# TensorE's scores in an inner loop with addresses computed up front, loops without `head_slot`, and an identity matmul moved ahead, in a decode-attention kernel

## The chip, the cores and the metric

The kernel runs on one core of one Trainium2 chip. The metric is the device time of one execution in microseconds (us), as the median of several runs. All runs quoted here are of the fast state, with a granted TensorE clock of 1.0. A profiled span is about 1.3 us shorter than the device time of the same run.

## The reference

One query per head attends to 65,536 keys: 32 query heads share 8 key and value heads, of dimension 128, in bf16.

```python
B, Hq, Hkv, Sq, Sk, D = 1, 32, 8, 1, 65536, 128
def reference(q, k, v):
    k = jnp.repeat(k, rep, axis=1)          # rep = 4
    v = jnp.repeat(v, rep, axis=1)
    scores = jnp.einsum("bhqd,bhkd->bhqk", q, k) * D ** -0.5
    p = _softmax(scores, axis=-1)
    return jnp.einsum("bhqk,bhkd->bhqd", p, v)
```

K and V together are 268 MB, and every byte is used once.

## The kernel before

K and V are cut into 16 tiles each (N = 16; two tiles per head), of 8.39 MB. The kernel keeps two K tiles and one V tile on the chip. SyncE issues the loads. A K tile may be loaded when VectorE has transposed the tile that lay there, and a V tile when TensorE has finished the product with the V tile before (PV).

```python
def load_k(i):
    if i >= NK: sp.wait_ge(tr_s, (i - NK + 1) * G)
    ...
def load_v(i):
    if i < N - HALVED:
        if i >= 1: sp.wait_ge(pv_s, 2 * i)
        load(vbuf, vf, i, 0, T, v_in)
        return
    ...                                      # the last two tiles are loaded in halves and pieces
load_k(0)
for j in range(1, N + 1):
    if j < N: load_k(j)
    load_v(j - 1)
```

On TensorE a turn of the loop makes the scores of tile `it`, 16 groups of 16 products, all unrolled, then the 256 small products with V of tile `it - 1`. `head_slot` in the head of a loop asks for a place for the loop's first instruction, slot 0 here; all three compute engines use it.

```python
with nc.Fori(0, N + 1, 1, engines=..., head_slot={pe.engine: 0}) as it:
    ...
    with pe.If_lt(turn, N):
        for g in range(G):
            if g % GU == 0: pe.wait_ge(mv_s, it * U + (g // GU + 1))
            pe.wait_ge(tr_s, it * G + (g + 1))
            scores(g, qcols)                 # 16 matmuls
    with pe.If_eq(skip, 0):
        pe.wait_ge(ex_s, it * R); pe.wait_ge(v_in, whole_ * 16)   # cut
        values(range(TH)); ...               # PV
pe.wait_ge(tail_s, 2)
pe.matmul(acc[:, 0:R], lhsT=ident, rhs=o2, start=False, stop=False)   # fp32 identity, in the tail
for n, a, b in list(pieces(VLAST, TH))[-NEND:]:                        # last 16 and 8 tiles of V
    pe.wait_ge(vlast_in[n], 16)
    values(range(a, b))
# VectorE and ScalarE:
with nc.Fori(0, H, 1, engines=..., head_slot={dv.engine: 0}) as h: ...
with nc.Fori(0, H, 1, engines=..., head_slot={ac.engine: 0}) as h: ...
```

Of the kernel before, what the change touches and what calls it, by code (L numbers as in the profile page):

```python
# [5 lines left out]
DT = mybir.dt  # L6
AF = mybir.ActivationFunctionType
ALU = mybir.AluOpType
AX = mybir.AxisListType

P = 128
S4 = 32
T = 256
TG = 16
G = T // TG
U = 4
GU = G // U
NK = 2
NKT = 2
FIRST = (64, 64, 128)  # L20
KLAST = (128, 128)
VLAST = (72, 32, 16, 8)
NEND = 2
HALVED = 2


# [8 lines left out]
def bass_standalone__gqa_softmax__decode_kernel(nc, q, k, v, out):  # L35
    B, Hq, Sq, D = q.shape
    _, H, Sk, _ = k.shape
    R = Hq // H
    CK = P * T
    assert B == 1 and Sq == 1 and D == P and Hq == H * R == S4 and R == 4  # L40
    C = Sk // CK
    assert Sk % CK == 0 and C == 2
    N = H * C
    A = P // S4
    NB, NE = 2, 2
    W = T // U * R
    TH = T // 2
    QH = NB * NE * A * R
    scale = float(D) ** -0.5
    TE = sum(VLAST[-NEND:])  # L50
# [6 lines left out]
    S = es.enter_context  # L57
# [6 lines left out]
    ktb = [sb(f"ktb{i}", [P, TG * D], DT.bfloat16) for i in range(NKT)]  # L64
    scs = sb("scs", [P, T * R], DT.float32)
    pts = sb("pts", [P, T * R], DT.bfloat16)
    qblk = sb("qblk", [P, H * QH], DT.bfloat16)
# [14 lines left out]
    dif, wgt, rhead, lsum, recip, o1, o2 = (cols(R) for _ in range(7))  # L82
# [5 lines left out]
    q4, qt = (scs[:, i * D // 2:(i + 1) * D // 2].bitcast(DT.bfloat16) for i in range(2))  # L88
    ident = ktb[0][:, 0:2 * P].bitcast(DT.float32)

    qkb = [S(nc.psum_tensor(f"qkb{i}", [P, 512], DT.float32)) for i in range(U)]
    acc = S(nc.psum_tensor("acc", [P, 512], DT.float32))

    def sem(name):
# [19 lines left out]
    def pieces(sizes, at=0):  # L114
        for n, size in enumerate(sizes):
            yield n, at, at + size
            at += size
# [66 lines left out]

    @block.tensor
    def _(pe):
        def scores(g, qcols):


            kt = ktb[g % NKT][:, :].rearrange("p (b n e) -> p b e n", b=NB, e=NE)  # L190
            for n in range(TG // A):
                at = (g % GU * (TG // A) + n) * A * R
                for be in range(NB * NE):
                    ins = pe.matmul(  # L194
                        qkb[g // GU][:, at:at + A * R],
                        lhsT=kt[:, be // NE, be % NE, n * P:(n + 1) * P],
                        rhs=qblk[:, bass.ds(qcols[be], A * R)],
                        start=be == 0, stop=be == NB * NE - 1,
                    )
            ins.then_inc(qk_s, 1)  # L200

        def values(tiles):

            for t in tiles:
                ins = pe.matmul(  # L205
                    acc[:, 0:R], lhsT=vbuf[:, t * D:(t + 1) * D], rhs=pts[:, t * R:(t + 1) * R],
                    start=t == 0, stop=t == T - 1,
                )
                if t % TH == TH - 1:
                    ins.then_inc(pv_s, 1)  # L210


        turn, skip, skipl, late, last, kept, whole = (
            pe.alloc_register(name) for name in ("turn", "skip", "skipl", "late", "last", "kept", "whole"))
        pe.reg_mov(turn, 0)
        pe.wait_ge(qb_s, A * NB)
        with nc.Fori(
            0, N + 1, 1, engines=bass.OrderedEngineSet([pe.engine]), head_slot={pe.engine: 0},
        ) as it:
            pe.reg_alu(skip, it, 1, ALU.is_lt)  # L220
            pe.reg_alu(last, it, N, ALU.is_ge)
            pe.reg_alu(late, it, N - HALVED + 1, ALU.is_ge)
            pe.reg_add(skipl, skip, last)
            pe.reg_alu(kept, it, N - 1, ALU.min)
            pe.reg_alu(whole, it, N - HALVED, ALU.min)
            kept_ = pe.snap(kept, min_val=0, max_val=N - 1)
            whole_, late_, last_ = (pe.snap(r, min_val=0, max_val=N) for r in (whole, late, last))
            hq = kept_ // C * QH
            qcols = [hq + be * A * R for be in range(NB * NE)]
            with pe.If_lt(turn, N):  # L230
                for g in range(G):
                    if g % GU == 0:
                        pe.wait_ge(mv_s, it * U + (g // GU + 1))
                    pe.wait_ge(tr_s, it * G + (g + 1))
                    scores(g, qcols)
            with pe.If_eq(skip, 0):
                pe.wait_ge(co_s, it - 1)
                pe.wait_ge(ex_s, it * R)
                pe.wait_ge(v_in, whole_ * 16)
                pe.wait_ge(va_in, late_ * 16 + last_ * 16)  # L240
                values(range(TH))
                pe.wait_ge(vb_in, late_ * 16)
                for n, a, b in list(pieces(VLAST, TH))[:-NEND]:
                    pe.wait_ge(vlast_in[n], last_ * 16)
                    values(range(a, b))
            with pe.If_eq(skipl, 0):
                values(range(T - TE, T))
            pe.reg_add(turn, turn, 1)


        pe.wait_ge(tail_s, 2)
        pe.wait_ge(ow_s, H)
        pe.matmul(acc[:, 0:R], lhsT=ident, rhs=o2, start=False, stop=False)  # L253
        for n, a, b in list(pieces(VLAST, TH))[-NEND:]:
            pe.wait_ge(vlast_in[n], 16)
            values(range(a, b))

    @block.vector
    def _(dv):
# [47 lines left out]
            dv.alloc_register(name) for name in ("started", "before", "filled", "last"))  # L307


        with nc.Fori(0, H, 1, engines=bass.OrderedEngineSet([dv.engine]), head_slot={dv.engine: 0}) as h:  # L310
            dv.reg_alu(started, h, 1, ALU.is_ge)
            dv.reg_alu(last, h, H - 1, ALU.is_ge)
            dv.reg_alu(filled, h, 1, ALU.add)
            dv.reg_alu(filled, filled, H - 1, ALU.min)
            dv.reg_alu(before, h, -1, ALU.add)
            dv.reg_alu(before, before, 0, ALU.max)
            started_, last_ = dv.snap(started, min_val=0, max_val=1), dv.snap(last, min_val=0, max_val=1)
            filled_, before_ = dv.snap(filled, min_val=0, max_val=H - 1), dv.snap(before, min_val=0, max_val=H - 2)
            for b in range(C):
                dv.wait_ge(k_in[b], (filled_ if b else h) * 16)  # L320
                moved = h * (C * U) + (U + b * U + 1)
                for g in range(G):
                    for n, at, _ in pieces(KLAST if b else FIRST):
                        if at == g * TG:
                            dv.wait_ge((klast_in if b else first_in)[n], last_ * 16 if b else 16)
                    if b * G + g >= NKT:
                        dv.wait_ge(qk_s, h * (C * G) + (b * G + g - NKT + 1))  # L327
                    else:
                        dv.wait_ge(qk_s, h * (C * G) - started_ * (NKT - 1 - g))  # L329
                    transpose(b, g)  # L330
                    if g >= 2 * GU and g % GU == 0:
                        maximum(b, g // GU - 2, moved)
                for u in range(U - 2, U):
                    maximum(b, u, moved)
                dv.wait_ge(mx_s, h * (C * U) + (b + 1) * U)
                if b:
                    dv.wait_ge(hma_s, h * C + 1)
                dv.tensor_reduce(  # L338
                    hmax[:, b * R:(b + 1) * R], hp[b].rearrange("p (u g) -> p g u", g=R), AX.X, ALU.max,
                ).then_inc(hm_s, 1)  # L340
                if b:
                    dv.wait_ge(hma_s, h * C + 2)
                    dv.tensor_tensor(dif, mfirst, mtot, ALU.subtract).then_inc(df_s, 1)  # L343
                    dv.wait_ge(pv_s, h * (2 * C) + 2)
                    dv.tensor_copy(o1, acc[:, 0:R]).then_inc(co_s, 1)  # L345
                else:
                    with dv.If_eq(started, 1):
                        weigh(before_)
                        dv.wait_ge(pv_s, h * (2 * C))
                        dv.wait_ge(ow_s, h)  # L350
                        dv.tensor_tensor(o2, acc[:, 0:R], o2, ALU.add).then_inc(co_s, 1)  # L351
                        divisor(before_)
                        dv.wait_ge(co_s, h * C)
                        dv.tensor_tensor(oT[:, bass.ds(before_ * R, R)], o2, recip, ALU.mult).then_inc(fin_s, 1)  # L354
# [9 lines left out]
    def _(ac):  # L364
# [4 lines left out]
        ac.activation(warm[:, 8:9], warm[:, 9:10], AF.Exp, scale=1.0).then_inc(warm_s, 1)  # L369

        def move(b, u):
            fr = qkb[u][:, 0:W].rearrange("p (n a g) -> p a n g", a=A, g=R)
            to = scs[:, u * W:(u + 1) * W].rearrange("p (n x g) -> p x n g", x=A, g=R)
            for x in range(A):
                for a in range(A):
                    ins = ac.activation(to[a * S4:(a + 1) * S4, x, :, :], fr[x * S4:(x + 1) * S4, a, :, :], AF.Copy)  # L376
            ins.then_inc(mv_s, 1)


        with nc.Fori(0, H, 1, engines=bass.OrderedEngineSet([ac.engine]), head_slot={ac.engine: 0}) as h:  # L380
            for b in range(C):
                ac.wait_ge(ex_s, h * (C * R) + b * R)
                for u in range(U):
# [49 lines left out]
```

## Time and profile before

| | before |
|---|---|
| time, median of 3 runs | 629.17 us (629.02 to 629.17) |
| span of the profiled run | 628.1 us |
| last V data landed (trace) | 625.04 us |
| first transpose of K on VectorE | 18.54 us |
| second V load issued | 78.1 us |

These are lines of the profile's page: busy time by engine, the span in 40 slices with the load rate, and the DMA queues (packets, MB, share of the 16 DMA engines' time). The queues marked "instruction" carry the instruction fetches. In the packet records of the span those of q8 have 16 KB and take 0.97 to 1.07 us, those of q14 have 8 KB and take 0.31 to 0.32 us. A fetch, or a block, is below one such packet. I put q8 down to TensorE and q14 to the other engines.

```profile
span 628.1 us, 19282 instructions
PE 269.9 (43%) x8194; PEld 243.9 (39%) x8194; DVE 341.2 (54%) x411; ACT 275.6 (44%) x1178; POOL 10.5 (2%) x32
...
DMA  9999999999999999999999999999999999999997
GB/s 368 438 449 424 439 422 413 455 413 451 417 451 417 451 417 442 426 442 426 438 430 438 430 434 434 434 434 434 430 438 430 438 430 430 438 415 430 434 432 293
...
q1 hardware_dynamic: 5892, 268.45, 99.1%
q8 instruction: 5, 0.08, 0.1%
...
q14 instruction: 5, 0.04, 0.0%
```

The DMA engines are busy from the first slice to the last, and no compute engine is busy much over half of the time. From the landing times of the loads, a tile takes 19.35 us in steady state. That is 8.389 MB / 19.35 us = 433.5 GB/s.

The waits of VectorE for its transposes (total us, times, longest):

```profile
DVE ktb L276 <- DMA kbuf<-in_k_dram: 142.3, 16, 11.5
...
DVE ktb L276 <- PE qkb L194: 7.0, 1, 7.0
DVE ktb L276 <- issue: 6.0, 1, 6.0
```

VectorE waits for data in every tile (16 waits, 142.3 us in all): here the loads set the pace. The other two waits come once each, near the start. The 6.0 us lie before the first transpose, and an 8 KB block is fetched within them, at 16.0 us (0.31 us).

The window from 78 to 81 us, where the second V load is issued (the last number is GB/s):

```profile
core 0: us, PE busy (x) PEld busy (x) DVE busy (x) ACT busy (x) POOL busy (x), PEclk, DMA share, GB/s
78.00:81.00 3.00, 0.04 (x2) 0.00 (x0) 0.16 (x1) 2.92 (x8) 0.00 (x0) 1.00 0.79 284
```

The chain of waits from 564 us to the end (start, length, what):

```profile
574.46 30.99 DMA vbuf<-in_v_dram
...
605.49 3.59 PE acc L205 x128
...
609.47 13.69 DMA vbuf<-in_v_dram
...
623.20 1.01 PE acc L205 x32
624.21 0.02 issue
624.23 0.56 PE acc L253 x2
624.79 0.69 PE acc L205 x24
```

The 0.56 us piece is the identity matmul. It sits on the drawn chain, but the last 8 of the 24 products behind it have to wait for data that landed at 625.04 us.

The trace records 16 increments of a load's semaphore, and the page counts 16 DMA engines; I read each increment as the landing of one DMA engine's share. The 16 times of a load then show how far the DMA engines are apart. For the second K tile they run from 41.64 to 43.80 us: the last DMA engine is 2.16 us behind the first. Below, this distance is called the lag. The times carry no name of a DMA engine, so "the last" is whichever one comes last in a load.

### The profile page before, as it was taken

How to read it: one execution, taken by the hardware profiler on the slowest of the kernel's cores; microseconds unless marked ns; L12 is line 12 of the kernel's file. 1: busy time of each engine (PE TensorE's matmuls, PEld its weight loads, DVE VectorE, ACT ScalarE, POOL GpSimd, SP SyncE). 2: the span in 40 equal slices, each digit the busy share in tenths (PEclk: the TensorE clock that was granted, in tenths of full speed). 3: DMA queues.
4: the chain of work that ended last, by engine and by line, in shares of the span. 5: the costliest groups of instructions: out<-in, count | busy, mean ns of one | idle time of the engine just before them, and what ended most of it. 6: DMA issues, size and time to landing. Idle time of an engine off the chain costs nothing.

```text
span 628.1 us, 19282 instructions
## 1 busy us (share of the span) xinstructions
PE 269.9 (43%) x8194; PEld 243.9 (39%) x8194; DVE 341.2 (54%) x411; ACT 275.6 (44%) x1178; POOL 10.5 (2%) x32
## 2 busy tenths in 40 slices
PE   0323737144361534615346252452615526156445
PEld 0312636044361433614335152452514526146444
DVE  1865576290753908538094480935719357195910
ACT  0363645164351734517346172461725526264640
POOL 0000000000000000000000000000000000000000
DMA  9999999999999999999999999999999999999997
GB/s 368 438 449 424 439 422 413 455 413 451 417 451 417 451 417 442 426 442 426 438 430 438 430 434 434 434 434 434 430 438 430 438 430 430 438 415 430 434 432 293
DMA packets 6094, 268.60 MB, mean 428 GB/s; under 512 B 964, under 2 KB 964, under 8 KB 1220
## 3 DMA queue, kind: packets, MB, share of 16 engines
q1 hardware_dynamic: 5892, 268.45, 99.1%
q8 instruction: 5, 0.08, 0.1%
q10 hardware_dynamic: 192, 0.03, 0.0%
q14 instruction: 5, 0.04, 0.0%
HBM read 268.47 MB, written 0.01 MB: 427 GB/s over the span
## 4 chain that ended last, share of the span: by engine, by line
DMA 63%; DVE 16%; issue 10%; PE 10%; DVEq 0%; SPq 0%; ACTq 0%
DMA kbuf<-in_k_dram 55%; DVE ktb L276 14%; PE acc L205 9%; DMA vbuf<-in_v_dram 7%; DVE small L283 1%; DMA scs<-in_q_dram 1%; PE qkb L194 1%; SPq L124 0%; ACTq L366 0%; DVE qblk L271 0%; DVEq L329 0%; DVEq L327 0%; PE acc L253 0%; DVE scs L263 0%; DVE oTX L361 0%
## 5 line engine op out<-in xcount | busy, mean ns | idle before, releaser
L276 DVE STREAM_TRANSPOSE ktb<-kbuf 128x1024 int32<-128x1024 int32 x256 | 295.7, 1212 | 155.8 <-DMA kbuf<-in_k_dram 142.3
L376 ACT ACTIVATE scs<-qkb 32x64 f32<-32x64 f32 x1024 | 220.3, 215 | 280.2 <-PE qkb L194 269.0
L194 PE MATMUL qkb<-qblk,ktb 128*128 x4096 | 157.1, 176 | 341.4 <-DVE ktb L276 326.4
L194 PEld LDWEIGHTS qkb<-qblk,ktb 128*128 128x128 bf16 x4096 | 132.7, 105 | 365.7 <-issue 202.6
L205 PE MATMUL acc<-pts,vbuf 128*128 128x4 bf16 x4096 | 112.4, 166 | 14.1 <-DMA vbuf<-in_v_dram 13.4
L205 PEld LDWEIGHTS acc<-pts,vbuf 128*128 128x128 bf16 x4096 | 111.0, 104 | 15.7 <-DMA vbuf<-in_v_dram 11.6
L283 DVE TENSOR_REDUCE small<-scs 128x4 f32<-128x256 f32 x64 | 37.5, 586 | 61.4 <-ACT scs L376 61.4
L399 ACT ACTIVATE pts<-scs,small 128x256 bf16<-128x256 f32 x64 | 48.9, 853 | 30.7 <-PE acc L205 30.5
L171 POOL PARTITION_ALL_REDUCE small<-small x16 | 5.9, 370 | 589.9 <-DVE small L338 589.9
L399 ACT ACTIVATION_READ_ACCUMULATOR pts<-scs,small 128x1 f32 x64 | 13.6, 213 | 0.0
L387 ACT ACTIVATE small<-small 128x4 f32<-128x4 f32 x16 | 3.3, 206 | 22.5 <-POOL small L171 22.5
L345 DVE COPY small<-acc 128x4 f32<-128x4 f32 x8 | 1.3, 161 | 19.4 <-PE acc L205 19.4
L351 DVE TENSOR_TENSOR small<-acc,small 128x4 f32<-128x4 f32 x7 | 1.1, 163 | 13.8 <-PE acc L205 13.8
L359 DVE TENSOR_TENSOR oTX<-acc,small 128x4 bf16<-128x4 f32 x1 | 0.2, 163 | 12.3 <-PE acc L205 12.3
L263 DVE STREAM_TRANSPOSE scs<-scs 128x64 int32<-128x64 int32 x1 | 0.2, 246 | 9.8 <-DMA scs<-in_q_dram 9.8
L338 DVE TENSOR_REDUCE small<-small 128x4 f32<-128x16 f32 (+1 forms) x16 | 3.0, 185 | 1.3
L163 POOL PARTITION_ALL_REDUCE small<-small x8 | 3.4, 429 | 11.5 <-DVE small L296 11.5
L343 DVE TENSOR_TENSOR small<-small 128x4 f32<-128x4 f32 x8 | 1.3, 163 | 4.0 <-POOL small L171 4.0
L294 DVE TENSOR_TENSOR small<-small 128x4 f32<-128x4 f32 x8 | 1.3, 163 | 2.7 <-ACT pts L399 2.7
L369 ACT ACT_TABLE_LOAD x1 | 1.3, 1283 | 3.1 <-issue 3.1
L354 DVE TENSOR_TENSOR oTX<-small 128x4 f32 x7 | 1.1, 163 | 1.7 <-DVE small L300 1.7
L292 DVE TENSOR_TENSOR small<-small 128x4 f32<-128x4 f32 x8 | 1.4, 181 | 0.9
(18 smaller groups left out, 8.8 us busy)
## 6 DMA issues: line engine op xcount, KB each, us to landing
kbuf<-in_k_dram SPq DMA_DIRECT2D x3, 4096.0 KB, 40.2
vbuf<-in_v_dram SPq DMA_DIRECT2D x3, 4096.0 KB, 24.7
kbuf<-in_k_dram SPq DMA_DIRECT2D x2, 2048.0 KB, 10.3
vbuf<-in_v_dram SPq DMA_DIRECT2D x1, 2304.0 KB, 11.6
vbuf<-in_v_dram SPq DMA_DIRECT2D x1, 1024.0 KB, 13.7
vbuf<-in_v_dram SPq DMA_DIRECT2D x1, 512.0 KB, 14.5
vbuf<-in_v_dram SPq DMA_DIRECT2D x1, 256.0 KB, 14.6
kbuf<-in_k_dram SPq DMA_DIRECT2D x14, 49.8
```

The source lines that it names most:

```text
L163: g.partition_all_reduce(lsum, rhead, P, bass.bass_isa.ReduceOp.add).then_inc(ls_s, 1)
L171: g.partition_all_reduce(mtot if b else mfirst, hmax[:, b * R:(b + 1) * R], P, bass.bass_isa.ReduceOp.max,).then_inc(hma_s, 1)
L194: ins = pe.matmul(qkb[g // GU][:, at:at + A * R], lhsT=kt[:, be // NE, be % NE, n * P:(n + 1) * P], rhs=qblk[:, bass.ds(qcols[be], A * R)] ...
L205: ins = pe.matmul(acc[:, 0:R], lhsT=vbuf[:, t * D:(t + 1) * D], rhs=pts[:, t * R:(t + 1) * R], start=t == 0, stop=t == T - 1,)
L276: dv.transpose(to.rearrange("p (b t j) -> p b t j", b=NB, t=TG), fr.rearrange("p (t b i) -> p b t i", b=NB, t=TG),).then_inc(tr_s, 1)
L283: dv.tensor_reduce(hp[b][:, u * R:(u + 1) * R], scs[:, u * W:(u + 1) * W].rearrange("p (n g) -> p g n", g=R), AX.X, ALU.max,).then_inc(mx_ ...
L292: dv.tensor_tensor(o2, o1, wgt, ALU.mult).then_inc(ow_s, 1)
L294: dv.tensor_tensor(rhead, rsum[0], wgt, ALU.mult).then_inc(rw_s, 1)
L338: dv.tensor_reduce(hmax[:, b * R:(b + 1) * R], hp[b].rearrange("p (u g) -> p g u", g=R), AX.X, ALU.max,).then_inc(hm_s, 1)
L376: ins = ac.activation(to[a * S4:(a + 1) * S4, x, :, :], fr[x * S4:(x + 1) * S4, a, :, :], AF.Copy)
L387: ac.activation(negb[b], mtot if b else mfirst, AF.Copy, scale=-scale).then_inc(nb_s, 1)
L399: ac.activation(pv[:, g_, :], sv[:, g_, :], AF.Exp, bias=negb[b][:, g_:g_ + 1], scale=scale, accum_out=rsum[b][:, g_:g_ + 1],).then_inc(ex ...
```

## The change

The intent was to shrink TensorE's program: the scores become an inner loop of 8 turns with two groups each, and the addresses of a turn are put into registers before its first wait. An empty first turn of the outer loop walks through the code while the data is still on its way. `head_slot` is gone from all three loops; VectorE's and ScalarE's then stay where they fall. The identity matmul moves from the tail into the middle of the last PV.

```diff
-qkb = [S(nc.psum_tensor(f"qkb{i}", [P, 512], DT.float32)) for i in range(U)]
+qkb = S(nc.psum_tensor("qkb", [P, U * BANK], DT.float32))
 ...
-        with nc.Fori(0, N + 1, 1, engines=..., head_slot={pe.engine: 0}) as it:
-            with pe.If_lt(turn, N):
-                for g in range(G):
-                    if g % GU == 0:
-                        pe.wait_ge(mv_s, it * U + (g // GU + 1))
-                    pe.wait_ge(tr_s, it * G + (g + 1))
-                    scores(g, qcols)
+        with nc.Fori(0, N + 2, 1, engines=engines) as it:
+            with pe.If_eq(skipk, 0):
+                addresses(qs)
+                with nc.Fori(0, G // NKT, 1, engines=engines) as gp:
+                    outs = [products(at + n * TG * R) for n in range(NKT)]
+                    addresses(sum(outs, []))
+                    pe.wait_ge(mv_s, kb_ * U + (upto + 1))
+                    for n in range(NKT):
+                        pe.wait_ge(tr_s, kb_ * G + (gp * NKT + (n + 1)))
+                        scores(ktb[n], outs[n], qs)
 ...                                    # PV in four parts, each under its own If
+                        with pe.If_eq(last, 1):
+                            pe.wait_ge(tail_s, 2)
+                            pe.wait_ge(ow_s, H)
+                            pe.matmul(acc[:, 0:R], lhsT=ident, rhs=o2, start=False, stop=False)
-        pe.wait_ge(tail_s, 2)
-        pe.wait_ge(ow_s, H)
-        pe.matmul(acc[:, 0:R], lhsT=ident, rhs=o2, start=False, stop=False)
 ...
-        with nc.Fori(0, H, 1, engines=..., head_slot={dv.engine: 0}) as h:
+        with nc.Fori(0, H, 1, engines=...) as h:
-        with nc.Fori(0, H, 1, engines=..., head_slot={ac.engine: 0}) as h:
+        with nc.Fori(0, H, 1, engines=...) as h:
```

More of the change, by code (lines that the diff above doesn't have):

```diff
@@ L23 @@
 NEND = 2
+BANK = 512
+PVIF = 4
 HALVED = 2
@@ L186, in _, with addresses, products, scores @@
     def _(pe):
-        def scores(g, qcols):
-            kt = ktb[g % NKT][:, :].rearrange("p (b n e) -> p b e n", b=NB, e=NE)
-            for n in range(TG // A):
-                at = (g % GU * (TG // A) + n) * A * R
-                for be in range(NB * NE):
+        def addresses(aps):
+            for ap in aps:
+                pe.lower_ap(ap)
+        def products(at):
+            return [qkb[:, bass.ds(at + n * A * R, A * R)] for n in range(TG // A)]
+        def scores(kt, outs, qs):
+            kt = kt[:, :].rearrange("p (b n e) -> p b e n", b=NB, e=NE)
+            for n, o in enumerate(outs):
+                for be, q_ in enumerate(qs):
                     ins = pe.matmul(
-                        qkb[g // GU][:, at:at + A * R],
-                        lhsT=kt[:, be // NE, be % NE, n * P:(n + 1) * P],
-                        rhs=qblk[:, bass.ds(qcols[be], A * R)],
+                        o, lhsT=kt[:, be // NE, be % NE, n * P:(n + 1) * P], rhs=q_,
                         start=be == 0, stop=be == NB * NE - 1,
@@ L210, in values @@
                     ins.then_inc(pv_s, 1)
-        turn, skip, skipl, late, last, kept, whole = (
-            pe.alloc_register(name) for name in ("turn", "skip", "skipl", "late", "last", "kept", "whole"))
-        pe.reg_mov(turn, 0)
-        pe.wait_ge(qb_s, A * NB)
-        with nc.Fori(
-            0, N + 1, 1, engines=bass.OrderedEngineSet([pe.engine]), head_slot={pe.engine: 0},
-        ) as it:
-            pe.reg_alu(skip, it, 1, ALU.is_lt)
-            pe.reg_alu(last, it, N, ALU.is_ge)
-            pe.reg_alu(late, it, N - HALVED + 1, ALU.is_ge)
-            pe.reg_add(skipl, skip, last)
-            pe.reg_alu(kept, it, N - 1, ALU.min)
-            pe.reg_alu(whole, it, N - HALVED, ALU.min)
-            kept_ = pe.snap(kept, min_val=0, max_val=N - 1)
-            whole_, late_, last_ = (pe.snap(r, min_val=0, max_val=N) for r in (whole, late, last))
-            hq = kept_ // C * QH
-            qcols = [hq + be * A * R for be in range(NB * NE)]
-            with pe.If_lt(turn, N):
-                for g in range(G):
-                    if g % GU == 0:
-                        pe.wait_ge(mv_s, it * U + (g // GU + 1))
-                    pe.wait_ge(tr_s, it * G + (g + 1))
-                    scores(g, qcols)
-            with pe.If_eq(skip, 0):
-                pe.wait_ge(co_s, it - 1)
-                pe.wait_ge(ex_s, it * R)
-                pe.wait_ge(v_in, whole_ * 16)
-                pe.wait_ge(va_in, late_ * 16 + last_ * 16)
-                values(range(TH))
-                pe.wait_ge(vb_in, late_ * 16)
-                for n, a, b in list(pieces(VLAST, TH))[:-NEND]:
-                    pe.wait_ge(vlast_in[n], last_ * 16)
-                    values(range(a, b))
@@ new lines, in _ @@
+        engines = bass.OrderedEngineSet([pe.engine])
+        turn, skip, skipk, skipl, late, last, kb, vb, whole = (
+            pe.alloc_register(name)
+            for name in ("turn", "skip", "skipk", "skipl", "late", "last", "kb", "vb", "whole"))
+        with nc.Fori(0, N + 2, 1, engines=engines) as it:
+            pe.reg_add(turn, it, 0)
+            pe.reg_alu(skip, it, 2, ALU.is_lt)
+            pe.reg_alu(last, it, N + 1, ALU.is_ge)
+            pe.reg_alu(skipk, it, 1, ALU.is_lt)
+            pe.reg_add(skipk, skipk, last)
+            pe.reg_alu(late, it, N - HALVED + 2, ALU.is_ge)
+            pe.reg_add(skipl, skip, last)
+            pe.reg_alu(kb, it, -1, ALU.add)
+            pe.reg_alu(kb, kb, 0, ALU.max)
+            pe.reg_alu(kb, kb, N - 1, ALU.min)
+            pe.reg_alu(vb, it, -1, ALU.add)
+            pe.reg_alu(vb, vb, 0, ALU.max)
+            pe.reg_alu(whole, vb, N - HALVED, ALU.min)
+            kb_ = pe.snap(kb, min_val=0, max_val=N - 1)
+            vb_, whole_, late_, last_ = (pe.snap(r, min_val=0, max_val=N) for r in (vb, whole, late, last))
+            with pe.If_eq(skipk, 0):
+                pe.wait_ge(qb_s, A * NB)
+                hq = kb_ // C * QH
+                qs = [qblk[:, bass.ds(hq + be * A * R, A * R)] for be in range(NB * NE)]
+                addresses(qs)
+                with nc.Fori(0, G // NKT, 1, engines=engines) as gp:
+                    upto = gp // (GU // NKT)
+                    at = gp * (NKT * TG * R) + upto * (BANK - W)
+                    outs = [products(at + n * TG * R) for n in range(NKT)]
[4 more added lines that the diff above has]
+                        scores(ktb[n], outs[n], qs)
+            parts = [range(n * T // PVIF, (n + 1) * T // PVIF) for n in range(PVIF)]
+            parts[-1] = range(parts[-1][0], T - TE)
+            for n, part in enumerate(parts):
+                with pe.If_eq(skip, 0):
+                    if n == 0:
+                        pe.wait_ge(co_s, vb_ - 1)
+                        pe.wait_ge(ex_s, vb_ * R)
+                        pe.wait_ge(v_in, whole_ * 16)
+                        pe.wait_ge(va_in, late_ * 16 + last_ * 16)
+                    if part[0] == TH:
+                        pe.wait_ge(vb_in, late_ * 16)
+                        with pe.If_eq(last, 1):
+                            pe.wait_ge(tail_s, 2)
+                            pe.wait_ge(ow_s, H)
+                            pe.matmul(acc[:, 0:R], lhsT=ident, rhs=o2, start=False, stop=False)
+                    at = part[0]
+                    for m, a, b in list(pieces(VLAST, TH))[:-NEND]:
+                        if a in part:
+                            values(range(at, a))
+                            pe.wait_ge(vlast_in[m], last_ * 16)
+                            at = a
+                    values(range(at, part[-1] + 1))
@@ L246, in _ @@
             with pe.If_eq(skipl, 0):
                 values(range(T - TE, T))
-            pe.reg_add(turn, turn, 1)
-        pe.wait_ge(tail_s, 2)
-        pe.wait_ge(ow_s, H)
-        pe.matmul(acc[:, 0:R], lhsT=ident, rhs=o2, start=False, stop=False)
         for n, a, b in list(pieces(VLAST, TH))[-NEND:]:
@@ L307, in _ @@
             dv.alloc_register(name) for name in ("started", "before", "filled", "last"))
-        with nc.Fori(0, H, 1, engines=bass.OrderedEngineSet([dv.engine]), head_slot={dv.engine: 0}) as h:
+        with nc.Fori(0, H, 1, engines=bass.OrderedEngineSet([dv.engine])) as h:
             dv.reg_alu(started, h, 1, ALU.is_ge)
@@ L371, in move @@
         def move(b, u):
-            fr = qkb[u][:, 0:W].rearrange("p (n a g) -> p a n g", a=A, g=R)
+            fr = qkb[:, u * BANK:u * BANK + W].rearrange("p (n a g) -> p a n g", a=A, g=R)
             to = scs[:, u * W:(u + 1) * W].rearrange("p (n x g) -> p x n g", x=A, g=R)
@@ L377, in move @@
             ins.then_inc(mv_s, 1)
-        with nc.Fori(0, H, 1, engines=bass.OrderedEngineSet([ac.engine]), head_slot={ac.engine: 0}) as h:
+        with nc.Fori(0, H, 1, engines=bass.OrderedEngineSet([ac.engine])) as h:
             for b in range(C):
```

## The prediction

> **What bounds the kernel.** The DMA engines. The page's slices show DMA busy 9 tenths throughout, 413 to 455 GB/s in the middle; from landing times one 8.39 MB tile takes 19.35 us (433.5 GB/s), so 32 tiles take 619 of the span's 628.1 us. [...] TensorE is busy 43%, VectorE 54%. The chain of waits names VectorE and TensorE only because their work ends in the next DMA issue; but a V load lands 31 us after its issue, a K load 50 us, against 19.35 us for its own bytes, so a V issue has about 11 us to spare. Compute is off the critical path except at the start and end.
>
> **What the change does.**
> 1. TensorE's 512 score instructions per tile become 64 in a loop of 8 turns, with an empty first outer turn. The DMA records show TensorE fetching five 16 KB instruction blocks (at 16.2, 31.6, 41.6, 48.6, 55.9 us, about 1.05 us each), and in the second tile VectorE waits 7.0 us once for scores. [...] I expect three or four, earlier.
> 2. [...] VectorE idles 6.0 us for "issue" from 12.5 us, with a fetch at 16.0. I expect the first transpose at 13 to 14 us.
> 3. Each pair of groups computes eight addresses and branches: estimate 0.5 to 1.5 us, from 0.046 us per register operation in the trace. TensorE's pair takes 1.2 us of VectorE's 2.3 to 2.8 us, so it is nearly hidden: at most 2 us later per tile.
> 4. The fp32 identity matmul (0.56 us in the tail) moves ahead. But the last 8 weight tiles start at 625.08, right after the last landing at 625.04: at most 0.05 us gained.
>
> **What is critical.** At 78.1 us V's second load is issued when only 2.3 us of earlier data are left for the fastest DMA engine; 78 to 81 us runs at 284 GB/s, losing about 1.0 us of mean engine time. With steps 1 and 2 the first PV ends some 6 to 12 us sooner and this dip goes. But the completion counts show the slowest engine already 2.1 us behind the fastest at 44 us, and it lost only about 0.15 us in the dip. The last engine decides, so I credit 0.1 to 0.3 us. At the end, V halves are issued with 1 to 3 us to spare (issue at 600.6, the load before landing 603.5 to 605.4 us), so a slower TensorE could cost up to 1 us.
>
> **Prediction.** 628.8 us, 8 in 10 between 627.9 and 629.9. Chances: faster by over 2% 0.01, within 2% 0.98, slower 0.01.
>
> **What would show it.** GB/s per slice unchanged after the sixth; V's second load issued before 73 us, without a dip; first transpose before 15 us; fewer 16 KB instruction packets; VectorE's wait for K near 140 us; last landing to the span's end still about 3 us.
>
> **What would make it wrong.** [...] more instruction packets, microseconds of "issue" per tile, single DMA engines delayed. Or addresses cost over 9 us per tile, and the DMA rate dips each period.

The marked gaps, here and in the expectations below, are statements that no trace or run of this case shows. 629.17 us, less 0.1 to 0.3 us for the dip and at most 0.05 us for the identity matmul, comes to 628.8 to 629.1 us, and 628.8 us was forecast. "Three or four" fetches in item 1 is the author's estimate, item 2 is about the two `head_slot`s that go from VectorE's and ScalarE's loops, and the first risk at the end is named only by its signs.

## The result, and the profile after

The kernel after takes 628.76 us (median of 6 runs, 628.59 to 628.82), the kernel before 629.17 us in the same rounds (629.02 to 629.63). The ratio is 0.9992, with a 95% interval of 0.9979 to 1.0005. A ratio is the mean time of one kernel's fast runs over that of the other's of the same rounds, so it is not quite the ratio of the medians. The ranges of the two kernels' six runs do not overlap, so about 0.4 us is there to be explained; two repeats in other rounds (runs 4 and 6 below) gave 0.56 and 0.52 us.

The same lines of the page:

```profile
span 627.5 us, 20255 instructions
PE 267.3 (43%) x8194; PEld 241.6 (39%) x8194; DVE 341.3 (54%) x411; ACT 274.8 (44%) x1178; POOL 10.5 (2%) x32
...
GB/s 368 439 456 414 455 414 455 414 451 414 451 418 451 418 451 418 443 426 434 434 426 439 418 451 409 460 409 460 409 460 409 460 409 460 409 428 434 434 432 276
...
q8 instruction: 2, 0.03, 0.0%
q14 instruction: 2, 0.02, 0.0%
```

The load rate is what it was (neighbouring slices trade some per cent, their mean does not move). Instruction fetches fell from ten to four: two of 16 KB for TensorE instead of five, and two of 8 KB for the others instead of five.

The waits of VectorE for its transposes; the two single waits are gone:

```profile
DVE ktb L303 <- DMA kbuf<-in_k_dram: 148.9, 17, 11.2
```

The window from 78 to 81 us: the second V load was issued at 71.2 us, and the dip is gone.

```profile
78.00:81.00 3.00, 0.00 (x0) 0.00 (x0) 0.00 (x0) 0.00 (x0) 0.00 (x0) 1.00 0.87 371
```

(A rate in so short a window jumps about: in windows of 1 us the kernel before shows 66 to 934 GB/s between 24 and 38 us. Most packets have 64 KB and take 2.42 us. The landing times decide, below.)

The chain of waits at the end:

```profile
574.30 30.63 DMA vbuf<-in_v_dram
...
605.32 3.58 PE acc L212 x128
...
609.77 14.10 DMA vbuf<-in_v_dram
...
623.92 0.59 PE acc L212 x16
...
624.55 0.39 PE acc L212 x8
```

The identity matmul has left the chain, and yet from the last landing to the end of the span it is 3.0 us, as before (625.04 to 628.06 us, now 624.51 to 627.51 us). So the whole gain of the profiled runs is in the last landing, 0.53 us earlier. The landing time of the last DMA engine shows where it arose:

| last DMA engine's landing, us | before | after | difference |
|---|---|---|---|
| second K tile | 43.80 | 43.51 | 0.29 |
| third K tile | 82.54 | 82.22 | 0.32 |
| second V tile | 102.07 | 101.56 | 0.51 |
| last piece of V | 625.04 | 624.51 | 0.53 |

0.32 us were there before the dip, 0.19 us came in it, and 0.02 us came in the following 520 us.

### The profile page after: what moved, and what is told of

The parts are those of the page before. It is cut to its first block, busy times and chain, and to the rows that moved or that the text cites. A ratio compares the mean times of both kernels' runs of the same rounds, so it can differ in the third digit from the quotient of the medians.

```text
span 627.5 us, 20255 instructions
## 1 busy us (share of the span) xinstructions
PE 267.3 (43%) x8194; PEld 241.6 (39%) x8194; DVE 341.3 (54%) x411; ACT 274.8 (44%) x1178; POOL 10.5 (2%) x32
## 4 chain that ended last, share of the span: by engine, by line
DMA 66%; DVE 15%; PE 9%; issue 9%; SPq 1%; DVEq 0%
DMA kbuf<-in_k_dram 58%; DVE ktb L303 14%; PE acc L212 9%; DMA vbuf<-in_v_dram 7%; DVE small L310 1%; PE qkb L203 1%; SPq L126 1%; DVEq L354 0%; DVEq L356 0%; DVE oTX L388 0%; DVE oTX L386 0%; DVEq L385 0%
## 5 line engine op out<-in xcount | busy, mean ns | idle before, releaser
L303 DVE STREAM_TRANSPOSE ktb<-kbuf 128x1024 int32<-128x1024 int32 x256 | 296.0, 1215 | 148.9 <-DMA kbuf<-in_k_dram 148.9
L203 PE MATMUL qkb<-qblk,ktb 128*128 x4096 | 152.2, 175 | 340.3 <-DVE ktb L303 311.0
L203 PEld LDWEIGHTS qkb<-qblk,ktb 128*128 128x128 bf16 x4096 | 129.2, 105 | 363.1 <-DVE ktb L303 363.1
L212 PE MATMUL acc<-pts,vbuf 128*128 128x4 bf16 x4096 | 114.7, 166 | 17.3 <-DMA vbuf<-in_v_dram 12.9
```

What stands on the lines that cost most here:

```text
L203: ins = pe.matmul(o, lhsT=kt[:, be // NE, be % NE, n * P:(n + 1) * P], rhs=q_, start=be == 0, stop=be == NB * NE - 1,)
L212: ins = pe.matmul(acc[:, 0:R], lhsT=vbuf[:, t * D:(t + 1) * D], rhs=pts[:, t * R:(t + 1) * R], start=t == 0, stop=t == T - 1,)
L303: dv.transpose(to.rearrange("p (b t j) -> p b t j", b=NB, t=TG), fr.rearrange("p (t b i) -> p b t i", b=NB, t=TG),).then_inc(tr_s, 1)
```

## The experiments

The theory after the result was this. Each DMA engine works through its share of the loads at a fixed pace of its own (19.35 us per tile). An instruction fetch takes one DMA engine away for a while; that engine is then behind for good, and the kernel ends with the DMA engine that is furthest behind. To this comes the dip of the late V load. The rivals were: the earlier start of the compute engines; the dip alone; the identity matmul. Every kernel gave a correct result. "Difference" is the kernel's median minus that of the kernel before in the same rounds; the kernel before took 629.29 to 629.48 us there.

**1. The kernel before without VectorE's and ScalarE's `head_slot`.** TensorE's program is the old one.

```diff
-with nc.Fori(0, H, 1, engines=..., head_slot={dv.engine: 0}) as h:
+with nc.Fori(0, H, 1, engines=...) as h:
-with nc.Fori(0, H, 1, engines=..., head_slot={ac.engine: 0}) as h:
+with nc.Fori(0, H, 1, engines=...) as h:
```

> The kernel before with the loop heads of VectorE and ScalarE left where they fall; TensorE untouched. Theory (the time is set by the DMA engine that instruction fetches and the one late V load put furthest behind): first transpose at 13 to 14 us instead of 18.5, but TensorE still fetches five 16 KB blocks, so V's second load is issued between 73 and 78 us and the dip there shrinks; last landing 0.0 to 0.3 us earlier; time 628.9 to 629.2. Rival (the start of the compute engines is what counts): the time falls by the whole 0.4 us, to 628.76.

Measured: 628.86 us, difference -0.47 us. These two small edits alone give the whole gain. My range was missed; the number is the rival's. The first transpose moved to 12.2 us and the V load to 75.6 us. TensorE still fetched five blocks of 16 KB, yet the last DMA engine was 1.58 us behind the first at the end, against 1.50 us in the kernel after with two: as I read it, TensorE's fetches fell on different DMA engines, so their number did not matter. The 16 landing times of the third K tile are the ground for this: nine lie within 0.35 us of each other, five are 1.3 to 1.4 us behind the median, and two are 0.9 to 1.0 us behind. That fits one DMA engine for each of the five fetches of 16 KB and the two of 8 KB.

**2. The kernel after with both heads put back**, so TensorE's part of the change alone.

> The kernel after with VectorE's and ScalarE's loop heads put back [...]; so TensorE's part of the change alone. Theory: first transpose back near 18 us, V's second load issued at about 75 us, still before the DMA queue runs dry, no dip; most of the gain stays: 628.7 to 628.95. Rival (early start of VectorE is what counts): back to 629.1.

Measured: 629.36 us, difference +0.03 us. The gain is gone. That again is the rival's number. But the trace does not fit the rival's reason: the V load was issued at 72.0 us, with no dip, so the early compute stages no longer delayed any load. What grew was the lag: 2.60 us when the first V tile landed and 2.29 us at the end, the worst of the kernels without padding. Of its five 8 KB fetches the one at 62.3 us raised the lag from 2.10 us (second K tile) to 2.60 us, and 2.45 us of it stayed. Here the fetches piled up: there were seven, as in run 1, but only four DMA engines are far behind at the third K tile (1.42 to 2.19 us behind the median).

**3. The kernel after with the identity matmul back in the tail.**

```diff
+        pe.wait_ge(tail_s, 2)
+        pe.wait_ge(ow_s, H)
+        pe.matmul(acc[:, 0:R], lhsT=ident, rhs=o2, start=False, stop=False)
         for n, a, b in list(pieces(VLAST, TH))[-NEND:]:
```

> The kernel after with the identity matmul back in the tail. Theory: the last 8 weight tiles wait for a landing, not for it; cost 0.0 to 0.1 us, 628.76 to 628.9. Rival (the 0.56 us that it took in the tail is what was gained): plus 0.4 to 0.55 us, 629.2 to 629.3.

Measured: 628.72 us, difference -0.61 us. Moving the matmul is worth nothing that these runs can see.

**4. and 5. The kernel after with the second V load issued later**, by an empty loop on SyncE before it (21 turns, then 30).

```diff
+                if i == 1:
+                    with nc.Fori(0, DELAY, 1, engines=bass.OrderedEngineSet([sp.engine])):
+                        sp.nop()
                 load(vbuf, vf, i, 0, T, v_in)
```

> The kernel after with V's second load issued some 7 us later (an empty loop on SyncE), near 78 us as in the kernel before. Theory: the dip at 78 to 81 us comes back (about 280 GB/s), the slowest DMA engine loses 0.1 to 0.3 us in it: 628.85 to 629.1. Rival 1 (the dip is the whole gain): 629.15 or more. Rival 2 (DMA engines that ran ahead lose it, the last loses nothing): 628.76.

The loop took less time than I had estimated: the load was issued at 76.4 us, 4.0 us before the first DMA engine ran out. Measured: 628.77 us, difference -0.56 us, and no dip. So this first attempt does not test the dip; it shows that 4.0 us of lead is enough.

> The kernel after with V's second load issued about 7.5 us later, near 78.6 us; the run before it delayed it to 76.4 us only, and no dip came. Theory: the dip at 78 to 81 us comes back; the DMA engines in front lose about 1 us, the last one, which is 1.6 us behind them, 0 to 0.2 us: 628.76 to 629.0. Rival (the dip costs its mean of about 1 us): 629.6 or more.

Measured: issued at 78.8 us, 1.7 us before the first DMA engine ran out; the dip came back (306 GB/s from 78 to 81 us); 630.35 us (629.71 to 630.98), difference +1.06 us. My theory missed. The profiled run, the fastest of the five, shows the last DMA engine taking 20.22 us from the third K tile to the second V tile (82.28 to 102.50 us) instead of 19.35 us: it lost 0.87 us, and the median one 1.1 us. In the kernel before, with the issue at 78.1 us, the last one lost 0.19 us. I had taken it that a DMA engine that is behind is spared; 0.7 us more of delay was enough to hit it. The trace's packet records show how: the new load's first packets start from 79.93 us on, just where the old load's end, but the first packet of 64 KB on each DMA engine took 2.55 to 3.71 us, against 2.42 us in run 4. In the kernel before it took 2.46 to 4.03 us. So the time was lost in slow first packets and not only in waiting for the load; why they are slow is open. Why the unprofiled runs lose up to another 1.3 us is open too. Run 11, below, adds a point: there the load was issued at 78.0 us, 2.4 us before the first DMA engine ran out, and the last one lost nothing.

**6. More fetches by an idle engine.** The first attempt put empty instructions on GpSimd.

> The kernel after with 256 empty instructions on the idle GpSimd after each of its first 15 reductions, which makes it fetch about 30 more 8 KB instruction blocks during the loads; no compute engine waits for them. Theory (a fetch delays the one DMA engine that carries it by 0.4 to 0.7 us, lasting, and the last DMA engine sets the time): if one sequencer's fetches keep to one DMA engine, its lag grows by about 0.5 us per fetch and the time by 8 to 16 us; if they rotate over the 16, every engine loses about 1 us and the time rises by 0.7 to 1.5 us. Rival (fetches matter only by making a compute engine start late): no change, 628.76.

The build dropped empty instructions: the trace has the 20255 instructions and the four fetches of the kernel after. So this is a repeat of the kernel after (628.77 us, difference -0.52 us) and no test.

**7. and 8. The same with instructions that add to a semaphore that nobody waits for.** PAD is 256 or 64.

```diff
+            for _ in range(PAD if n < N - 1 else 0):
+                g.nop().then_inc(pool_s, 1)
```

> The kernel after with 256 counting instructions (each adds one to a semaphore that nobody waits for) on the idle GpSimd after each of its first 15 reductions: 3840 instructions, about 30 more fetches of 8 KB during the loads. The first attempt used empty instructions, which the build dropped. Theory (a fetch delays for good the one DMA engine that carries it, by 0.4 to 0.7 us, and the last DMA engine sets the time): if one sequencer's fetches keep to one DMA engine, its lag grows by about 0.5 us per fetch and the time by 8 to 16 us; if they rotate over the 16, each loses about 1 us and the time rises by 0.7 to 1.5 us. Rival (fetches matter only when a compute engine starts late): 628.76.

> The same with 64 in place of 256: 960 instructions, 7 or 8 fetches. Theory: on one DMA engine they make a lag of about 4 us against the 1.5 us of the worst one now, so plus 2 to 3 us, 631 to 632; if they rotate, each adds 0.5 us to another DMA engine and the worst gains 0 to 0.6 us. Rival: 628.76.

Measured: 3840 instructions brought 30 more fetches of 8 KB (32 in q14 against 2), 960 brought 8 (10 against 2). The times are 647.31 us with 256 (difference +17.8 us) and 632.67 us with 64 (+3.2 us), both above my ranges. Load rate and instruction queue with 256:

```profile
GB/s 381 458 403 443 447 406 442 447 426 426 447 438 411 446 451 406 442 447 406 439 439 418 423 426 386 455 389 451 422 410 410 398 447 446 395 416 428 331 291 243
...
q14 instruction: 32, 0.26, 0.1%
```

and the queue with 64:

```profile
q14 instruction: 10, 0.08, 0.0%
```

0.26 MB of fetches, a thousandth of the data, cost 2.8% of the time. The landing times show why. With 64, one DMA engine falls back further and further (1.70 us behind at 121 us, 5.66 us at 609 us, with six fetches between), while the other 15 keep their places. That is (5.66 - 1.70) / 6 = 0.66 us per fetch of 8 KB. With 256, the lag of the last grows by 0.66 and 0.65 us per fetch around 90 and 120 us and from 350 us on stays between 11.0 and 12.4 us: there, as I read it, the other DMA engines have to wait for it, because further loads are issued only when whole tiles have landed and been used, and a V load is issued some 11 us ahead. From then on every fetch delays everything. So GpSimd's fetches here kept to one DMA engine and added up. The rival, that the padding made GpSimd's own results late, does not hold: ScalarE's waits for GpSimd are the same without padding and with 256 (total us, times, longest):

```profile
ACT small L414 <- POOL small L173: 22.4, 16, 1.5
```

```profile
ACT small L417 <- POOL small L174: 22.4, 16, 1.5
```

**9. and 10. One head at a time put back into the kernel after.**

> The kernel after with VectorE's loop head alone back [...]. Theory: two or three more 8 KB fetches, all on the DMA engine of VectorE's fetches; if that is also one that a TensorE fetch hit, its lag goes from 1.5 to 2.0 us or more and the time to about 629.1 to 629.4, else 628.76. With the next run it shows which of the two loop heads costs what.

> The kernel after with ScalarE's loop head alone back [...]. Theory: one or two more 8 KB fetches on the DMA engine of ScalarE's fetches; the first transpose stays near 13.5 us. 628.76 to 629.2; the two runs together should account for the 0.6 us of the run with both heads put back. Rival (VectorE's late start is what costs): this one stays at 628.76 and only the run with VectorE's head is slow.

Measured: VectorE's head alone 629.00 us, difference -0.48 us, with one more fetch; ScalarE's head alone 629.42 us, difference -0.06 us, with two more. Both ranges were missed: the first is below 629.1 to 629.4 us, the second above 628.76 to 629.2 us. Both forecasts took it that the fetches of one engine keep to one DMA engine; the runs show that for GpSimd (run 8) and not for these two. The waits of VectorE and the fetches, first with VectorE's head put back:

```profile
DVE ktb L303 <- issue: 5.2, 1, 5.2
```

```profile
q14 instruction: 3, 0.02, 0.0%
```

then with ScalarE's:

```profile
q14 instruction: 4, 0.03, 0.0%
```

With VectorE's head the first transpose is as late as in the kernel before (18.6 us), VectorE idles 5.2 us for it, and the kernel is still fast. With ScalarE's head VectorE starts at 13.6 us without that wait, and the kernel is slow. That speaks against the rival of the early start, which had the better numbers in runs 1 and 2. The lag of the last DMA engine at the end is 1.98 us and 2.13 us, in the order of the times. The ranges of five runs overlap (628.90 to 629.37, 629.14 to 629.88 us), so the split between the two heads is likely rather than certain.

Kernels in the order of the last landing, from one profiled run each:

| kernel | 8 KB and 16 KB fetches | last lag, us | last landing, us | difference of time, us |
|---|---|---|---|---|
| after, identity in the tail | 2, 2 | 1.61 | 624.25 | -0.61 |
| before, no heads on VectorE, ScalarE | 2, 5 | 1.58 | 624.28 | -0.47 |
| after, repeat (run 6) | 2, 2 | 1.78 | 624.44 | -0.52 |
| after | 2, 2 | 1.50 | 624.51 | -0.41 |
| after, VectorE's head | 3, 2 | 1.98 | 624.67 | -0.48 |
| after, ScalarE's head | 4, 2 | 2.13 | 624.82 | -0.06 |
| after, both heads | 5, 2 | 2.29 | 625.03 | +0.03 |
| before | 5, 5 | 1.88 | 625.04 | 0 |

The two profiles of the kernel after show how far single profiles can be trusted: their lags differ by 0.28 us, their last landings by 0.07 us. With 1.50 us the first DMA engines were themselves 0.3 us later. (Before has less lag at its end than in its first tiles because the dip cost the DMA engines in front up to 1.4 us and the last one 0.19 us.)

**11. and 12. TensorE held by an empty loop before PV**, first in all tiles but the last two, then in the last two alone.

```diff
                     if n == 0:
+                        with pe.If_eq(late, 0):            # run 12: late, 1
+                            with nc.Fori(0, DELAY, 1, engines=engines):
+                                pe.nop()
                         pe.wait_ge(co_s, vb_ - 1)
```

> The kernel after with TensorE held about 5 us by an empty loop before the PV of each of the first 14 tiles. Theory: a V load is then issued about 5 us later, with about 6 us to spare; no change, 628.7 to 628.9. Rival (TensorE's work is part of the critical chain, as the chain of waits draws it): plus 5 us per tile at most, 70 us.

Measured: 632.39 us, difference +3.10 us. TensorE was held for about 6.5 us per tile, 14 times, some 90 us in all, and every V tile up to 566 us landed within 0.2 us of where it does in the kernel after. VectorE's wait for K fell from 148.9 to 60.3 us: it took up the delay. The 3 us came at the end, where I had not looked far enough ahead: the held work pushed the PV of the next-to-last tile from 596.7 to 602.5 us, and the last tile's first half was issued at 606.1 instead of 600.3 us, after the load before it had landed.

> The kernel after with TensorE held about 3 us before the PV of the last two tiles only. Theory: the issue of the last tile's first half moves from 600.3 to about 603.3 us, where the DMA engines[...] have 0 to 1.6 us left: the load rate dips near 604 to 606 us and the time rises by 1.0 to 2.0 us. Rival (TensorE is off the critical path here as well): no change.

The gap is a time from issue to data that no trace shows. Measured: 630.94 us, difference +1.65 us, so about 2.1 us more than the kernel after (differences -0.41 to -0.52 us). The issue moved from 600.33 to 604.66 us, and the load rate fell:

```profile
602.00:604.00 2.00, 2.00 (x81) 2.00 (x79) 0.00 (x0) 0.00 (x0) 0.00 (x0) 1.00 0.12 49
604.00:606.00 2.00, 1.52 (x57) 1.44 (x55) 0.00 (x0) 0.00 (x0) 0.00 (x0) 1.00 0.81 229
```

4.3 us at this one load cost 2.1 us, while 90 us spread over the tiles before it cost nothing until they reached the same load. There TensorE is on the critical path, and in the tiles between the start and this load it is not.

## Why the prediction was right

- **The bound** was right. DMA rate and tile time did not move, and 90 us more on TensorE in 14 tiles moved the last landing of no tile before the end by more than 0.2 us (run 11).
- **The time** was right (628.8 predicted, 628.76 us measured), and "the last engine decides" was the sentence that carried it. That the two agree to 0.04 us is luck: the runs of one kernel differ by more, and the gains credited add up to 0.1 to 0.35 us only.
- **The signs** mostly came: V's second load at 71.2 us, without a dip (forecast: before 73 us), the first transpose at 13.6 us (13 to 14 us). TensorE fetched two 16 KB blocks, where three or four were estimated, and VectorE's wait for K was 148.9 us and not near 140 us.
- **The identity matmul** was right: at most 0.05 us was credited; the last landing to the end took 3.0 us in both, and putting it back cost nothing (run 3).
- **The addresses** were right: from the head of the inner loop to its first product TensorE spends about 1.0 us per pair in the trace (89.87 to 90.90 us in one turn), within the estimate of 0.5 to 1.5 us, and the last V half is issued at 600.33 us, no later than before.
- **The term that was mis-sized** is "With steps 1 and 2 the first PV ends some 6 to 12 us sooner and this dip goes ... I credit 0.1 to 0.3 us". The dip did go, and it was worth 0.19 us to the last DMA engine. But the larger part, 0.32 us, was there before the dip, in the lag that I had read from the landing times and had taken as given. I did not ask what makes the lag, nor that step 2, with fewer fetches, would lessen it.
- **Step 1's part** was credited and had none: TensorE's old program with five fetches reaches the same time (run 1), and its new program alone does not gain (run 2). The two heads on VectorE and ScalarE are the change; ScalarE's head is likely the larger part (runs 9 and 10).
- **The risk named**, more instruction packets, did not come: after 70 us none of the kernels without padding fetched anything (the last fetch is at 43.92 us in the kernel after, at 69.31 us in the kernel before).

Open is which DMA engine carries which sequencer's fetches: the landing times are not labelled by DMA engine, so I can see that one of them was hit again but not name it. Open is also what the dip costs: an issue at 78.0 us (run 11) lost the last DMA engine nothing, one at 78.1 us (before) 0.19 us, one at 78.8 us 0.87 us in the profiled run and more in others.

No version clearly beats the kernel after. Run 3 is as fast. By the lag at its end (1.50 us), up to 1.5 us might be won by having no DMA engine behind; this is an estimate, and no run shows it. Since one 16 KB fetch by itself put its DMA engine 1.3 to 1.4 us behind the median, as I read the landing times of run 1, the first thing to try would be a TensorE program that needs no fetch during the loads. I did not build one.

## What to carry to other kernels

When loads fill all DMA engines from start to end, look at how far apart they finish a load: the kernels of the table above ended with the last one, 1.50 to 2.29 us behind the first, and by an estimate from run 8 a fetch that puts one DMA engine 0.66 us behind early on costs up to 0.66 us at the end, if that is the engine that comes last and nothing in between makes all wait. Fetches that fell on different DMA engines, as the landing times of run 1 read, did not add up; fetches on one did (runs 2, 7 and 8). Count instruction fetches during the loads, by queue, before placing loop heads by `head_slot` or unrolling on an idle engine: both heads on VectorE and ScalarE brought three more fetches and 0.6 us (run 2), and 3840 useless instructions on an idle engine 30 more and 18 us. A compute engine off the critical path could be held for long in the middle of this kernel (some 90 us moved no landing up to 566 us by more than 0.2 us, run 11), but hardly where the last loads are issued (4.3 us cost 2.1 us, run 12).

## What the traces show of fetches and late loads

- TensorE's fetches had 16 KB (packets of 1.0 us), those of the others 8 KB (packets of 0.31 us).
- A fetch during the loads costs the data time: each 8 KB fetch in run 8 put its DMA engine 0.66 us behind, twice the 0.30 us that 8 KB take at a sixteenth of 433.5 GB/s. Against the kernel after (difference -0.52 us in its repeat), 30 such fetches cost 18.3 us (+17.8 us) and 8 of them 3.7 us (+3.2 us). An estimate from these runs fits: 30 or 8 times 0.66 us, less the 1.5 us by which the last DMA engine is behind anyway, is 18.3 and 3.8 us.
- GpSimd's fetches kept to one DMA engine (TensorE's five in run 1 did not, as I read the landing times): with 64 padding instructions per tile one DMA engine alone fell from 1.70 to 5.66 us behind.
- The lag lasts: 1.75 us at 102 us, still 1.58 us at 605 us in the kernel after.
- In run 12 the first packet of a load started 0.95 us after the start of the issuing instruction, in the kernel after that of the first load of all 0.99 us after it (0.75 to 1.74 us). A following load of 8.39 MB had to be issued earlier than that: with 4.0 us of data left for the first DMA engine nothing was lost, with 2.4 us (run 11) the median DMA engine lost 0.15 us, with 2.3 us (before) 1.4 us, with 1.7 us 1.1 us. Why the step is so sharp, and why these last two are not in order, is not settled.
